# Fused delta-rule attention and two mixture-of-experts layers: sums of weight quarters on VectorE, and a sparser, reordered weight preparation

## The chip, the cores and the metric

The kernel runs on one core of a Trainium2 chip. The metric is the device time of one execution in microseconds (us). The engines are named as the profile names them: PE is TensorE (matmuls; PEld its weight loads), DVE is VectorE, ACT is ScalarE, POOL is GpSimd, SP is SyncE, which issues most of the DMAs. Each engine works through a queue of its own in order.

## The reference

Three stages follow each other on 4 sequences of 768 tokens (3072 tokens, 384 features):

```python
for t in range(S):                                  # delta-rule attention, 8 heads of 48
    y[:, :, t] = q[:, :, t] @ state
    state = state + beta * outer(k_n[:, :, t], v[:, :, t] - k_n[:, :, t] @ state)
...
logits = x @ w_gate                                 # MoE 1: soft routing, Sinkhorn, 8 experts
P = exp(logits - logits.max())                      # 8 times normalised over rows and columns
for e in range(E):
    out += P[:, e:e + 1] * (maximum(x @ w1[e], 0.0) @ w2[e])
...
expert_idx = argmax(xn @ en.T / tau, axis=1)        # MoE 2: one expert for each token
for e in range(E):
    out[mask] = gate_w[mask, None] * (maximum(x[mask] @ w1[e], 0.0) @ w2[e])
```

w1 is 384 x 1024 and w2 is 1024 x 384 for each expert. MoE 1 sends every token through every expert.

## The kernel before

The program has three parts in time. Part 1 (0 to about 560 us) is the attention with the experts 0 and 1 of MoE 1 woven in; a scheduler class orders it. Part 3 (from about 1664 us) is expert 7 of MoE 1, the routing and MoE 2; the scheduler orders it too. The change touches neither. It touches part 2, the experts 1 (rest) to 6 of MoE 1, whose order is written out by hand:

- **Foreground.** Every fp32 value is held as two fp16 halves, high and low, and a product takes three matmuls (high x high, high x low, low x high). First come the last groups of expert 1 (`moe1_group`, `mlp1`, `mlp2`, run by `run`), where PE works on L468 (first layer) and L479 (second layer), DVE makes the low halves of the hidden values on L452 and adds results to `accb` on L494. Then come 60 **units**: 12 blocks of 256 tokens for each of the experts 2 to 6. A unit has a first half (`blocks_first`: four blocks of 18 matmuls, L534) and a second half (`blocks_second`: seven products of 12 matmuls, L584), made Strassen-like from quarters of the hidden block and of w2. `turned` interleaves the first half of unit u with the second half of unit u-1: block, two products, block, two products, block, two products, block, one product.
- **Work on DVE, ACT and POOL for a unit.** ACT makes relu and high halves (L542, L543, L519), DVE the low halves from PSUM (L544) and from SBUF (L522), POOL four sums of hidden quarters (L525), and DVE adds finished products into `accb` (L566, L570). A product whose operand or whose PSUM bank isn't ready stops PE, whose queue is in order.
- **Background.** `bg()` advances every queue in `bgs` by one step, that is, up to the next `yield`. While units run, `paced` calls `bg()` each time 1050 ns of nominal matmul time have been written (14 steps to a unit); before that `run` calls it at every second matmul group. What a step writes goes into the engines' queues at that place.
- **What the background does.** One queue holds `first_accs` and then two `woven_group`s, which weight and sum the parts of experts 0 and 1 into `accb` (L601, L602; L624, L626). The other, `prepq`, holds weight preparations and a small `setup2` for MoE 2: `prep1(e)` prepares expert e of MoE 1 (e = 2 is `first_prep`, with a staging buffer of its own), `prep2(e)` expert e of MoE 2, which it writes to `w2d` in DRAM. `prep2` waits until both woven groups are done, because they share a buffer. `prep1(e + 1)` enters the queue behind the job in progress when the first unit of expert e has been written.
- **A preparation (`prep_w`)** loads w1 and later w2 into `st` (L351, L353), takes sums of squares (ACT, L394), turns them into one power of two for all partitions (DVE L397 to L399; `over_parts`: DVE writes a diagonal on L358, PE multiplies it by ones on L362, DVE takes the maximum on L364), and then splits w1 or w2 into high and low halves by `split_steps`: ACT writes the high half of one piece (L371), DVE the low half of the piece before (L374), one such pair to a step. For w2 of the experts 2 to 6 of MoE 1 the pieces are `quarters`: three quarters of 128x768 are split, then four differences of quarters are formed in place on POOL (L431), then the four results are split. A quarter's split has 768 elements per partition, the other pieces have 512.
- **The end of part 2.** After the last unit's first half, its remaining high and low halves are written in one go, then its second half, then what is left in `bgs`.

## Time and profile before

| | us |
|---|---|
| runs (3) | 2100.07, 2102.55, 2106.96 |
| median | 2102.55 |
| the profiled execution: time | 2101.38 |
| the profiled execution: span from first to last instruction | 2099.2 |
| PE busy in the span | 1985.6 (95%) |
| DVE, ACT, POOL busy | 1387.7 (66%), 1150.6 (55%), 602.3 (29%) |
| part 2, 696 to 1664 us: length, PE busy | 968.0, 945.5 |

PE is the bound nearly everywhere, so the profile is read as a list of PE's idle times: which wait ended each of them, and what the engine that PE waited for was doing just before. The instruction durations of DVE, as listed, overlap the next one by about 0.07 us; the distance between the starts of two instructions in a row is what one really occupies.

### The profile page before, as it was taken

What the parts mean: (1) busy time and instruction counts of PE and PEld (TensorE: products, weight loads), DVE (VectorE), ACT (ScalarE), POOL (GpSimd) and SP (SyncE); (2) the same over time, 40 slices, a digit from 0 to 9 for tenths busy, and PEclk for the clock granted to TensorE, in tenths of its full rate; (3) what the DMA queues carried; (4) which work ended last, traced back from release to release, by engine and by line L of the source; (5) the groups of instructions that cost most, each with busy time, mean ns of one, the idle gap of its engine ahead of it and who ended that gap; (6) DMA issues with size and microseconds to landing.
All of it is one profiled execution on the core that took longest, in us unless ns stands there. A gap on an engine that the chain in (4) does not pass through costs nothing. (4 is left out here: it accounts for less than half of the span.)

```text
span 2099.2 us, 55384 instructions
## 1 busy us (share of the span) xinstructions
PE 1985.6 (95%) x23391; PEld 1630.9 (78%) x23391; DVE 1387.7 (66%) x3045; ACT 1150.6 (55%) x2374; POOL 602.3 (29%) x524
## 2 busy tenths in 40 slices
PE   3779999999999999999999999999999999999998
PEld 3667777777775479999899989988999755567777
DVE  6988988988772776776767677676766555551111
ACT  6766665666532656666666656665665333433322
POOL 2232233223100123533533343353333201022211
PEclk9889999999999999999999999999999999999999
DMA  8355655546535113022032112302220010168765
GB/s 281 82 104 107 126 114 110 123 103 132 116 100 208 45 61 121 32 92 91 31 121 96 58 54 99 121 32 91 95 88 31 1 28 20 31 222 332 251 222 208
DMA packets 325982, 230.02 MB, mean 110 GB/s; under 512 B 258572, under 2 KB 303536, under 8 KB 319330
## 3 DMA queue, kind: packets, MB, share of 16 engines
q1 hardware_dynamic: 321442, 216.18, 34.7%
q0 software_dynamic: 4288, 10.25, 1.4%
q8 instruction: 185, 3.03, 0.6%
q14 instruction: 67, 0.55, 0.1%
HBM read 146.94 MB, written 50.36 MB: 94 GB/s over the span
## 5 line engine op out<-in xcount | busy, mean ns | idle before, releaser
L534 PE MATMUL pt<-big,W 128*128 128x256 f16 x4320 | 511.0, 273 | 0.0
L534 PEld LDWEIGHTS <-W 128*128 128x128 f16 x4320 | 418.5, 98 | 43.9 <-issue 0.3
L542 ACT ACTIVATE R<-pt 128x512 f32<-128x512 f32 x240 | 142.6, 594 | 306.9 <-PE pt L534 283.4
L525 POOL TENSOR_TENSOR R<-R,R 128x512 f32<-128x512 f32 x120 | 155.3, 1294 | 371.6 <-ACT R L542 288.2
L566 DVE SCALAR_TENSOR_TENSOR accb<-py,pet,accb 128x192 f32<-128x192 f32 x240 | 123.0, 513 | 203.8 <-PE py L584 203.3
L525 POOL TENSOR_TENSOR R<-R 128x512 f32<-128x512 f32 x120 | 161.6, 1346 | 195.3 <-ACT R L542 190.6
L584 PEld LDWEIGHTS <-A 128*128 128x128 f16 x2520 | 211.1, 98 | 7.2 <-DVE A L522 2.6
L1089 PE MATMUL pt<-accb,W 128*128 128x256 f16 (+1 forms) x1368 | 180.9, 272 | 3.5 <-ACT accb L729 1.8
L1115 PE MATMUL py<-W,hhl 128*128 128x384 f16 x756 | 152.6, 328 | 2.6 <-ACT yo L1125 1.7
L584 PE MATMUL py<-W,A 128*128 128x192 f16 x1440 | 134.7, 246 | 2.1 <-DVE accb L566 1.4
L1089 PEld LDWEIGHTS <-W 128*128 128x128 f16 x1368 | 118.3, 100 | 18.7 <-issue 3.8
L1635 PEld LDWEIGHTS <-W 128*128 128x128 f16 x1008 | 90.6, 98 | 51.1 <-issue 0.7
L584 PEld LDWEIGHTS <-hhl 128*128 128x128 f16 x1440 | 120.6, 98 | 5.9 <-DVE hhl L522 3.6
L1655 PE MATMUL py<-W,hhl 128*128 128x384 f16 x624 | 108.8, 326 | 0.0
L1641 DVE SCALAR_TENSOR_TENSOR ttb<-pt,ttb 128x512 f16<-128x512 f32 x50 | 34.6, 692 | 111.5 <-ACT ttb L1640 111.1
L584 PE MATMUL py<-W,hhl 128*128 128x192 f16 x1080 | 105.1, 246 | 2.8 <-DVE hhl L522 2.7
L1115 PEld LDWEIGHTS <-hhl 128*128 128x128 f16 x864 | 74.2, 98 | 40.8 <-DVE hhl L1102 3.2
L394 ACT ACTIVATE jk<-st 128x512 f32<-128x512 f32 x162 | 98.0, 605 | 13.7 <-DMA st<-in_moe_w_dram 11.4
L584 PE MATMUL py<-ew,A 128*128 128x192 f16 x1080 | 104.3, 246 | 0.6 <-DVE A L522 0.5
L522 DVE TENSOR_TENSOR A<-R,A 128x512 f16<-128x512 f32 x120 | 100.7, 841 | 2.9 <-ACT A L519 2.9
L584 PEld LDWEIGHTS <-ttb 128*128 128x128 f16 x1080 | 91.0, 98 | 9.9 <-issue 5.4
L1635 PE MATMUL pt<-big,W 128*128 128x512 f16 x432 | 97.7, 379 | 0.0
(411 smaller groups left out, 4090.4 us busy)
## 6 DMA issues: line engine op xcount, KB each, us to landing
st<-in_moe_w_dram SPq DMA_DIRECT2D x27, 1536.0 KB, 9.9
W<-w2d SPq DMA_DIRECT2D x18, 1536.0 KB, 8.2
w2d<-big SPq DMA_DIRECT2D x16, 1536.0 KB
big<-w2d SPq DMA_DIRECT2D x8, 1536.0 KB, 7.4
accb<-w2d SPq DMA_DIRECT2D x8, 1536.0 KB, 8.1
big<-accb SPq DMA_DIRECT2D x90, 128.0 KB, 3.6
accb<-in_kq_dram SPq DMA_DIRECT2D x23, 448.0 KB, 4.6
st<-PTc SPq DMA_DIRECT2D x42, 128.0 KB, 3.2
```

The source lines that it names most:

```text
L394: nc.scalar.activation(out=jk, in_=st[:, c * CW:c * CW + CW], func=AF.Square, scale=2.0 ** 0.5, accum_out=ss[:, c:c + 1])
L522: return lambda: nc.vector.tensor_tensor(out=A[2 * k + 1], in0=src, in1=A[2 * k], op=ALU.subtract)
L525: nc.gpsimd.tensor_tensor(out=out, in0=a, in1=b, op=op)
L534: nc.tensor.matmul(out=po, lhsT=w1v(W, wv, kk, f), rhs=xv[:, kk].rearrange("p (h n) -> p h n", h=2), start=kk == 0 and x == 0 and f % 2 == ...
L542: nc.scalar.activation(out=(R1, R)[y][:, :, o:o + 256], in_=pv if y else pv_, func=AF.Relu)
L566: nc.vector.scalar_tensor_tensor(out=acc[t][:, sl], in0=src, scalar=sc, in1=acc[t][:, sl], op0=ALU.mult, op1=ALU.add)
L584: nc.tensor.matmul(out=py, lhsT=A[2 * ka + a_][:, 128 * q_:128 * q_ + 128], rhs=B[2 * kb + b_][:, DH * q_:DH * q_ + DH], start=first and q ...
L1089: nc.tensor.matmul(out=o[g4][:, nt_ * j:nt_ * j + nt_], lhsT=w1v(W, wv, kk, f_), rhs=XR[:, xv, kk], start=(kk == 0 and x == 0), stop=(kk = ...
L1115: nc.tensor.matmul(out=o["py", j][:, 0:DM], lhsT=a_[f_ // per][:, c_:c_ + 128], rhs=w2v(W, b_, f_), start=(f_ == 0 and x == 0), stop=(f_ = ...
L1635: nc.tensor.matmul(out=po, lhsT=w1v(W, wv, kk, f), rhs=xv[:, kk, :], start=(kk == 0 and x == 0), stop=(kk == KD - 1 and x == 2))
L1641: V((f"rs{q_}", id_), lambda q_=q_: nc.vector.scalar_tensor_tensor(out=HL[q_], in0=o[q_], scalar=0.0, in1=HH[q_], op0=ALU.max, op1=ALU.sub ...
L1655: nc.tensor.matmul(out=o["py"][:, 0:DM], lhsT=a_[f // per][:, c_:c_ + 128], rhs=w2v(W, b_, f), start=(f == 0 and x == 0), stop=(f == KF - ...
```

## The change

- The four differences of w2 quarters move from POOL (`gpsimd`) to DVE (`vector`), and the four empty steps behind them go.
- For experts 3 to 6 the quarter splits stand two steps apart instead of one (`more=1`); for expert 2 they stay one step apart.
- In `over_parts` the matmul comes one step later after the diagonal.
- In the woven groups each sum is followed by three steps instead of one, and the next load by ten instead of six. In `setup2` the transposes come two steps later.
- `prep1(3)` now stands in the queue right behind `setup2`, ahead of `prep2(0)`, and waits there until the first unit has been written (`open_`); the later ones enter as before.

```diff
--- before.py
+++ after.py
@@ -358,12 +358,13 @@
         nc.vector.tensor_scalar(out=dg, in0=I128, scalar1=m1, scalar2=c_, op0=ALU.mult, op1=ALU.mult)
         yield 1
         yield 1
+        yield 1
         pm = psm.tile([128, 128], F32, name="pmx", tag="m1")
         nc.tensor.matmul(out=pm, lhsT=one16, rhs=dg, start=True, stop=True)
         yield 1
         nc.vector.tensor_reduce(out=ma, in_=pm, op=ALU.max, axis=AX.X)
 
-    def split_steps(parts, s):
+    def split_steps(parts, s, more=0):
 
         for n_ in range(len(parts) + 1):
             if n_ < len(parts):
@@ -372,7 +373,8 @@
             if n_:
                 src, hi, lo = parts[n_ - 1]
                 nc.vector.scalar_tensor_tensor(out=lo, in0=src, scalar=s, in1=hi, op0=ALU.mult, op1=ALU.subtract)
-            yield 1
+            for _ in range(1 + more):
+                yield 1
 
     def prep_w(w1, w2, e, W, iv, stages, dst=None, wt=None, mats=None):
         half = WCOLS // 2
@@ -409,7 +411,7 @@
             else:
                 Wd, o = W, 0
             if i and mats is not None:
-                yield from quarters(st, mats, s)
+                yield from quarters(st, mats, s, 0 if apart_ else 1)
             else:
                 yield from split_steps([(st[:, c * CW:c * CW + CW], *(
                     Wd[:, wcol(i, c, part) - o:wcol(i, c, part) - o + CW] for part in range(2))) for c in range(NCH)], s)
@@ -419,20 +421,18 @@
         nc.vector.scalar_tensor_tensor(out=iv, in0=ps_[0], scalar=0.25, in1=ps_[1], op0=ALU.mult, op1=ALU.mult)
         yield 1
 
-    def quarters(st, mats, s):
+    def quarters(st, mats, s, more):
 
         q_ = st.rearrange("p (x f y d) -> p x y f d", x=2, f=FH, y=2)
         b11, b12, b21, b22 = (q_[:, x, y] for x in range(2) for y in range(2))
 
         def to(k, src):
             return (src, *(mats[2 * k + part].rearrange("p (f d) -> p f d", f=FH) for part in range(2)))
-        yield from split_steps([to(k, src) for k, src in enumerate((b11, b21, b22))], s)
+        yield from split_steps([to(k, src) for k, src in enumerate((b11, b21, b22))], s, more)
         for out, a, b in ((b11, b12, b11), (b12, b22, b12), (b22, b22, b11), (b21, b21, b22)):
-            nc.gpsimd.tensor_tensor(out=out, in0=a, in1=b, op=ALU.subtract)
+            nc.vector.tensor_tensor(out=out, in0=a, in1=b, op=ALU.subtract)
             yield 1
-        for _ in range(4):
-            yield 1
-        yield from split_steps([to(k, src) for k, src in ((3, b11), (5, b12), (4, b22), (6, b21))], s)
+        yield from split_steps([to(k, src) for k, src in ((3, b11), (5, b12), (4, b22), (6, b21))], s, more)
 
     def w1v(W, part, kk, f):
         o = (f // FH) * 3072 + part * 1536 + kk * 512 + (f % FH) * 128
@@ -625,12 +625,13 @@
             for x in range(2):
                 nc.vector.scalar_tensor_tensor(
                     out=acc[t], in0=yw[x, g][:, t % 4], scalar=pe[x][:, t:t + 1], in1=acc[t], op0=ALU.mult, op1=ALU.add)
-                yield 1
+                for _ in range(3):
+                    yield 1
             yield 1
         if g + 1 < GW:
             woven_load(0, y0d, g + 1)
             woven_load(1, y1d, g + 1)
-            for _ in range(6):
+            for _ in range(10):
                 yield 1
         woven[0] += 1
 
@@ -1446,8 +1447,8 @@
         yield 1
         er = yield from inv_norm(ess, 1, 8)
         nc.vector.tensor_scalar(out=ench, in0=ench, scalar1=er, scalar2=None, op0=ALU.mult)
-        yield 1
-        yield 1
+        for _ in range(4):
+            yield 1
         pt_ = psm.tile([128, KD, E], F32, name="pen", tag="m1")
         for kk in range(KD):
             nc.tensor.transpose(out=pt_[:, kk], in_=ench[:, 128 * kk:128 * kk + 128], identity=cs[0:8, 0:8])
@@ -1517,6 +1518,13 @@
     queue([], first_accs(), *(woven_group(g) for g in range(GW)))
     queue(prepq, iter([1] * 3), first_prep)
     queue(prepq, setup)
+    open_ = []
+
+    def prep1_3():
+        while not open_:
+            yield 1
+        yield from prep1(3)
+    queue(prepq, prep1_3())
     for e in range(E):
         queue(prepq, prep2(e))
     def paced(main, ns):
@@ -1581,8 +1589,10 @@
             paced(first_of(u), BGNS)
             paced(second_of(NG - 1), BGNS)
         if new_:
-            prepq.insert(min(1, len(prepq)), prep1(e + 1))
-            queue(prepq)
+            open_.append(e)
+            if e > 2:
+                prepq.insert(min(1, len(prepq)), prep1(e + 1))
+                queue(prepq)
     while early or late or lows:
         take(lows, early, late, late)
     paced(second_at(len(units) - 1), BGNS)
```

In the listings below, taken from the built programs, line numbers are those of each program's own file; in the changed one L375 is the low half of a split (L374 before), L433 the difference of quarters (L431), L421 the end of a preparation (L419). A row is operation, output<-inputs and size.

DVE, the last group of expert 1 before the units, where expert 2's w2 is prepared. `stb` is its staging buffer, W_96 its weights, `hhl` the hidden values, `py` the PSUM bank of a second-layer result. Before:

```order
L452 SCALAR_TENSOR_TENSOR hhl<-pt,hhl 128x512
L626 SCALAR_TENSOR_TENSOR accb<-big,pet,accb 128x384
L374 SCALAR_TENSOR_TENSOR W_96<-stb,w1s,W_96 128x768
L452 SCALAR_TENSOR_TENSOR hhl<-pt,hhl 128x512
L626 SCALAR_TENSOR_TENSOR accb<-big,pet,accb 128x384
L374 SCALAR_TENSOR_TENSOR W_96<-stb,w1s,W_96 128x768
L494 SCALAR_TENSOR_TENSOR accb<-py,pet,accb 128x384
L626 SCALAR_TENSOR_TENSOR accb<-big,pet,accb 128x384 x2
L494 SCALAR_TENSOR_TENSOR accb<-py,pet,accb 128x384
L626 SCALAR_TENSOR_TENSOR accb<-big,pet,accb 128x384
L494 SCALAR_TENSOR_TENSOR accb<-py,pet,accb 128x384
```

And now:

```order
L452 SCALAR_TENSOR_TENSOR hhl<-pt,hhl 128x512
L375 SCALAR_TENSOR_TENSOR W_96<-stb,w1s,W_96 128x768 x2
L494 SCALAR_TENSOR_TENSOR accb<-py,pet,accb 128x384
L626 SCALAR_TENSOR_TENSOR accb<-big,pet,accb 128x384
L375 SCALAR_TENSOR_TENSOR W_96<-stb,w1s,W_96 128x768
L433 TENSOR_TENSOR stb<-stb 128x4x192
L494 SCALAR_TENSOR_TENSOR accb<-py,pet,accb 128x384
L433 TENSOR_TENSOR stb<-stb 128x4x192 x2
L494 SCALAR_TENSOR_TENSOR accb<-py,pet,accb 128x384
L626 SCALAR_TENSOR_TENSOR accb<-big,pet,accb 128x384
L433 TENSOR_TENSOR stb<-stb 128x4x192
L494 SCALAR_TENSOR_TENSOR accb<-py,pet,accb 128x384
```

The third split, the differences (four L433, before on POOL) and the splits behind them stand between the L494 rows, and three of the five L626 shown (the woven sums) have gone further back; the last L452 of the group stands ahead of all splits.

In the units, at the differences for expert 4: POOL before (L525 are the unit's own sums, R its hidden blocks):

```order
L525 TENSOR_TENSOR R_15165<-R_15165 128x512
L431 TENSOR_TENSOR st<-st 128x4x192 x4
L525 TENSOR_TENSOR R_15165<-R_15165,R 128x512
L525 TENSOR_TENSOR R<-R,R_15165 128x512
L525 TENSOR_TENSOR R<-R 128x512
```

DVE before, from a unit's first L566 through the second group of splits:

```order
L566 SCALAR_TENSOR_TENSOR accb<-py,pet,accb 128x192
L522 TENSOR_TENSOR hhl<-R_15165,hhl 128x512
L544 SCALAR_TENSOR_TENSOR A_15162<-pt,A_15162 128x256
L522 TENSOR_TENSOR ttb<-R,ttb 128x512
L374 SCALAR_TENSOR_TENSOR W_96<-st,w1s,W_96 128x768
L374 SCALAR_TENSOR_TENSOR ew_14615<-st,w1s,ew_14615 128x768
L566 SCALAR_TENSOR_TENSOR accb<-py,pet,accb 128x384
L522 TENSOR_TENSOR ttb<-R,ttb 128x512
L374 SCALAR_TENSOR_TENSOR ew_14615<-st,w1s,ew_14615 128x768
L566 SCALAR_TENSOR_TENSOR accb<-py,pet,accb 128x192
```

DVE now, at the differences:

```order
L375 SCALAR_TENSOR_TENSOR W_96<-st,w1s,W_96 128x768
L570 SCALAR_TENSOR_TENSOR accb<-py,pet,accb 128x384
L544 SCALAR_TENSOR_TENSOR A_15158<-pt,A_15158 128x2x256
L433 TENSOR_TENSOR st<-st 128x4x192 x3
L566 SCALAR_TENSOR_TENSOR accb<-py,pet,accb 128x192
L433 TENSOR_TENSOR st<-st 128x4x192
L522 TENSOR_TENSOR A_15158<-R_15160,A_15158 128x512
L544 SCALAR_TENSOR_TENSOR hhl<-pt,hhl 128x256
L522 TENSOR_TENSOR A_15158<-R,A_15158 128x512
```

The differences have left POOL's queue, where they stood ahead of a unit's sums, and three stand on DVE in a row and a fourth behind one L566, all ahead of the two L522 that make the next operands.

DVE at the end of part 2, the last unit. L570 adds the last product of the unit before. Before:

```order
L566 SCALAR_TENSOR_TENSOR accb<-py,pet,accb 128x384
L522 TENSOR_TENSOR ttb<-R_15165,ttb 128x512
L544 SCALAR_TENSOR_TENSOR hhl<-pt,hhl 128x2x256
L570 SCALAR_TENSOR_TENSOR accb<-py,pet,accb 128x384
L544 SCALAR_TENSOR_TENSOR hhl<-pt,hhl 128x2x256
L522 TENSOR_TENSOR hhl<-R_15165,hhl 128x512
L522 TENSOR_TENSOR ttb<-R,ttb 128x512 x2
L566 SCALAR_TENSOR_TENSOR accb<-py,pet,accb 128x192
L566 SCALAR_TENSOR_TENSOR accb<-py,pet,accb 128x384
```

And now:

```order
L375 SCALAR_TENSOR_TENSOR big<-st,w1s,big 128x512 x3
L566 SCALAR_TENSOR_TENSOR accb<-py,pet,accb 128x384
L522 TENSOR_TENSOR ttb<-R_15161,ttb 128x512
L544 SCALAR_TENSOR_TENSOR hhl<-pt,hhl 128x2x256
L375 SCALAR_TENSOR_TENSOR big<-st,w1s,big 128x512 x2
L570 SCALAR_TENSOR_TENSOR accb<-py,pet,accb 128x384
L544 SCALAR_TENSOR_TENSOR hhl<-pt,hhl 128x2x256
L375 SCALAR_TENSOR_TENSOR big<-st,w1s,big 128x512
L522 TENSOR_TENSOR hhl<-R_15161,hhl 128x512
L522 TENSOR_TENSOR ttb<-R,ttb 128x512 x2
L566 SCALAR_TENSOR_TENSOR accb<-py,pet,accb 128x192
```

Six splits of the last preparation, `prep2(7)`, now stand between the last unit's rows, one of them just ahead of its L522; before, that preparation had ended nearly four units earlier.

## Rows read from the trace of the kernel before

**Rows 1.** Part 2 as one stretch: length, busy us (x instructions) by engine, PE's clock, DMA.

```profile
696.00:1664.00 968.00, 945.53 (x9663) 864.83 (x9662) 679.36 (x1217) 593.38 (x1250) 358.89 (x260) 1.00 0.20 72
```

**Rows 2.** PE's waits in 696:1664: who waited for whom, total us, times, longest.

```profile
PE py L584 <- DVE accb L566: 5.9, 6, 1.8
PE pmx L362 <- DVE btok L358: 3.6, 8, 1.2
PE py L479 <- DVE hhl L452: 2.8, 1, 2.8
...
PE pen L1453 <- DVE yo L1448: 1.4, 1, 1.4
```

**Rows 3.** Stretches of the quarter preparations, experts 2 to 6 (engines PE, PEld, DVE, ACT, POOL).

```profile
720.00:740.00 20.00, 15.00 (x81) 7.67 (x80) 17.81 (x21) 7.90 (x14) 7.62 (x4) 1.00 0.10 29
873.50:896.50 23.00, 23.00 (x245) 21.69 (x243) 21.13 (x29) 14.61 (x24) 16.73 (x9) 1.00 0.01 2
1004.50:1029.50 25.00, 22.91 (x237) 20.65 (x236) 22.53 (x28) 14.82 (x25) 14.95 (x9) 1.00 0.01 2
1200.50:1225.50 25.00, 22.28 (x229) 20.05 (x228) 22.43 (x28) 14.30 (x25) 15.72 (x9) 1.00 0.01 2
1396.50:1421.50 25.00, 22.28 (x232) 20.45 (x229) 22.13 (x28) 13.62 (x23) 16.64 (x10) 1.00 0.00 1
```

**Rows 4.** Timeline of DVE, four places: start, duration, what, how many.

```profile
720.39 1.02 DVE L374 SCALAR_TENSOR_TENSOR W<-stb,w1s,W 128x768 f16<-128x768 f32 x1
...
723.64 2.56 DVE L374 SCALAR_TENSOR_TENSOR W<-stb,w1s,W 128x768 f16<-128x768 f32 x1
...
728.71 4.02 DVE L626 SCALAR_TENSOR_TENSOR accb<-big,pet,accb 128x384 f32<-128x384 f32 x2
...
843.48 0.68 DVE L522 TENSOR_TENSOR ttb<-R,ttb 128x512 f16<-128x512 f32 x1
844.08 0.28 DVE L364 TENSOR_REDUCE w0p<-pmx 128x1 f32<-128x128 f32 x1
...
1014.55 2.05 DVE L522 TENSOR_TENSOR ttb<-R,ttb 128x512 f16<-128x512 f32 x1
1016.52 0.68 DVE L544 SCALAR_TENSOR_TENSOR hhl<-pt,hhl 128x512 f16<-128x512 f32 x1
...
1605.94 0.15 DVE L419 SCALAR_TENSOR_TENSOR ivt<-w0p,w1p 128x1 f32<-128x1 f32 x1
```

**Rows 5.** Timeline of POOL, two of these places (in brackets: idle before, and releaser).

```profile
721.50 3.89 POOL L431 TENSOR_TENSOR stb<-stb 128x768 f32<-128x768 f32 x2 [114.78 <-DVE W L374]
728.43 3.88 POOL L431 TENSOR_TENSOR stb<-stb 128x768 f32<-128x768 f32 x2 [3.04 <-DVE W L374]
...
1014.24 1.81 POOL L431 TENSOR_TENSOR st<-st 128x768 f32<-128x768 f32 x1 [0.96 <-DVE W L374]
```

**Rows 6.** Timeline of PE, three places; its listed ends are modelled.

```profile
726.86 4.24 PE L479 MATMUL py<-W,hhl 128*128 128x384 f16 x25 [2.79 <-DVE hhl L452]
...
838.17 1.15 PE L584 MATMUL py<-ew,hhl 128*128 128x192 f16 x12
839.16 2.13 PE L534 MATMUL pt<-big,W 128*128 128x256 f16 x18
841.13 0.66 PE L584 MATMUL py<-W,hhl 128*128 128x192 f16 x6
842.18 0.23 PE L362 MATMUL pmx<-btok,c 128*128 128x128 bf16 x1 [0.39 <-DVE btok L358]
...
1656.93 1.00 PE L584 MATMUL py<-W,hhl 128*128 128x192 f16 x10 [0.90 <-DVE hhl L522]
1659.76 1.15 PE L584 MATMUL py<-ew,ttb 128*128 128x192 f16 x12 [1.83 <-DVE accb L566]
```

**Rows 7.** Groups by line and shape in part 2: count, busy us, mean ns, idle before.

```profile
L525 POOL TENSOR_TENSOR R<-R 128x512 f32<-128x512 f32 x120 | 161.6, 1346 | 195.3 <-ACT R L542 190.6
...
L374 DVE SCALAR_TENSOR_TENSOR W<-st,w0s,W 128x512 f16<-128x512 f32 x36 | 25.5, 743 | 1.9 <-ACT W L371 1.7
```

## Prediction

> **What bounds the kernel now.** I read the stretches first. Part 2, all that the change touches, lasts 968.0 us, of which PE works 945.5 [rows 1]; its clock is granted in full. So nothing here can give more than 22.5 us. Then PE's waits in that part [rows 2]: every large one is for DVE. Those for L358 are scattered over the preparations, those for L452 and for the constants of MoE 2 (L1453) stand before the units or in the first one. Most of the rest lies in the stretches where quarters of w2 are prepared [rows 3]: there PE loses 5.0 us (20.00 less 15.00) for expert 2, nothing for 3, then 2.1, 2.7 and 2.7 for 4 to 6, 12.5 us in all. DVE is busy 88 to 92% in these stretches, POOL 60 to 73% in the four inside the units.
>
> Why DVE is late there is seen instruction by instruction. A quarter's low half takes 1.02 us alone and 2.56 beside POOL's differences; two L626 take 4.02 [rows 4] while POOL runs two differences in 3.9 [rows 5]. For expert 4, POOL starts a difference at 1014.24 and ends at 1016.05; L522, begun at 1014.55, lasts until 1016.60, as if it had begun when POOL ended [rows 4, 5]. The Trainium skill ("SBUF — State Buffer", SBUF: two separate sides) says that the port pair which these two engines share is an exclusive lock, held for a whole instruction; this trace agrees, with 2.05 us against 0.68.
>
> So PE pays less for DVE's own work than for DVE held up behind POOL, and for unit sums (L525) held up in POOL's queue behind the differences.
>
> **What the change costs and gives, part by part.** In a row of DVE an instruction occupies about 0.07 us less than is listed: L522 at 843.48 lists 0.68, the next begins 0.60 later [rows 4]. I use such occupancies: L522 and L452 0.60, a quarter split 0.93, L494, L626 and L566 of full width 0.53 (listed 0.6).
>
> *A difference on DVE* doesn't occur before. Lower bound: L522 is the same operation with 512 elements, 0.60 free; a split costs 1.02 - 0.743 = 0.28 more with 768 elements than with 512 [rows 4, 7]; so 0.87. Upper bound: held up for a whole unit sum of POOL, 1.35 [rows 7], so 2.2. I take 0.87 where POOL's queue has nothing, and up to 1.8 where the order puts it beside unit sums.
>
> *Expert 2.* No units run yet, so POOL, rid of the differences, does nothing, and all of DVE is at free prices. In the order now the last L452 stands ahead of all splits, so the 2.79 us wait for it [rows 6] goes. After it, up to the second L494, DVE has three splits, two L494, one L626 and one difference: 2.8 + 1.6 + 0.9 = 5.3 us. PE needs the bank that this L494 frees for its fourth result, that is, three results after it began the first (2.0 us each: 25 matmuls in 4.24 [rows 6]), 5.9. DVE starts on this row some 1.5 us after PE begins the first, so PE waits 5.3 + 1.5 - 5.9 = 0.9. From there to the first L452 of the next group stand three differences 2.6, two L494 and two L626 2.1, two splits 1.9 and L452 0.6, 7.2 us, against 5.9 until PE needs what it frees: 1.3. So 2.2 remain of 5.0. Bounds 1 and 4. **Gain 2.8.**
>
> *Experts 3 to 6.* Two opposite things: seven splits and all unit sums lose POOL's differences, and splits stand two steps apart; but DVE gets four differences in four steps. I add up DVE's row from the order and compare with the moment at which PE wants the operand: a block of 18 takes 1.97 us (839.16 to 841.13), a product 0.99 [rows 6]. Expert 4, shown above: at the unit's start the three unit sums run on POOL, 4 us. DVE's L570 and L544 end 1.2 us in, the first difference is held up to 2.9, the next two end at 4.2 and 5.1, L566 at 5.4, the fourth at 6.3, L522 at 6.9. Its operand is wanted after a block, two products and a block, in the third matmul: 6.1. PE waits 0.8 to 0.9. The same sum for experts 3, 5 and 6, where the differences stand elsewhere in the unit, gives 0.5, 0.8 and 0.65. To each I add a margin of 0.4 for what the sum leaves out between engines: 4.5 remain of 7.5. Lower bound 0.5 in all (no difference meets a unit sum); upper bound 22 (in each stretch two more differences and one or two splits are held up by a whole unit sum, 2.6 + 1.8, all of it on PE). I take 4.5, because POOL without differences has four unit sums of 1.3 us in a unit of 14.8, a third of the time [rows 7]. **Gain 3.0.**
>
> *The diagonal's product one step later.* PE waited eight times for L358, 3.6 us, at most 1.2 [rows 2]. A step is 1.05 us of matmuls, so the unit's own matmuls cover all but 0.15 of each; what comes behind, the maximum and the splits, has no deadline. Were the cover gone, the 3.6 would stay. **Gain 3.3.** The transposes of `setup2` come two steps later: the 1.4 us wait [rows 2] goes, **1.4**.
>
> *Woven sums spread out.* Sixteen L626 as before, eleven of them now in the first units, where 0.53 us each mostly fits into DVE's gaps; some stand beside the splits of `prep1(3)`'s w1. Between 0 and 1.5; **cost 0.3**.
>
> *Preparations that wait, and added steps.* `open_` is a matter of the order in which the program is written; no engine waits on it. Behind it stands `prep2(0)`, which nobody needs before part 3, and expert 3 is needed only twelve units later. `prep1(3)` loads some 1.5 us later than `prep2(0)` did, with nothing on SP's queue that PE needs sooner; 26 products and four quarter sequences (9 steps more, 4 fewer) add 46 steps of 1.05 us: 50 us in all. Before, the last preparation ended at 1605.9 [rows 4], 58 us ahead of the units' end near 1664, so it still ends inside. But its last six splits now stand in the last unit (order, above), where PE already waits 0.90 and 1.83 us for L522 and L566 [rows 6]. The split just ahead of L522 costs DVE 0.67 to 1.8, partly while it would have waited for POOL's sums anyway. **Cost 0.6** (0 to 2).
>
> *The splits of 512 elements.* Part of the wait for L566 [rows 2] belongs to them, and hangs on where in a unit they fall; the added step moves each half by one. I expect as many as before: 0, with 2 either way.
>
> Sum: 2.8 + 3.0 + 3.3 + 1.4 - 0.3 - 0.6 = 9.6 us. Against the profiled execution, 2101.4, that is 2091.8; it lay 1.2 below the median of the runs, so I forecast 2093.0 (0.45% less).
>
> **The rivals.**
>
> *A. DVE becomes the bound in the quarter stretches.* It is 88 to 92% busy there [rows 3] and gets more to do. At the upper bound experts 3 to 6 cost 22 us in place of 7.5; expert 2 still gives 2.0, L358 and L1453 give 4.7, the end takes 2: 9.8 slower, 2112. It is slower than before from 3.1 us to a stretch, by over 0.3% from 4.6. For: for expert 4 the order puts three differences right behind the unit sums. Against: a split alone takes 1.02, and POOL's share falls from two thirds to a third.
> A rule of the Trainium skill ("Perfetto Trace Analysis", Optimizing Scalar/DVE Operations) speaks for A: where DVE is saturated, it may pay to offload work to other engines, GpSimd included, though it warns that these two share a port. By its first half the differences belong on POOL and the sum is A's; by the rows on the lock it is the forecast's.
>
> *B. The place of the wait moves, its size stays.* The four differences take on DVE what the lock gave back, so in the units 7.5 stay, while expert 2, L358 and L1453 give 6 and the end takes 1.5: 2098, within 0.3%.
>
> *C. Nearly all of these stalls go:* no difference meets a unit sum. 4 + 7 + 3.5 + 1.4 = 16 us, 2086.5.
>
> **How the numbers follow.** A measurement of this kernel can tell 0.3%, 6.3 us, from no change; so faster means below 2096.2. Forecast (2089 to 2096) 0.45, B (2096 to 2104) 0.32, A 0.09, C 0.14. The range leaves out A, a tail of B and half of C: 2086 to 2103. Faster: the forecast's and C's, 0.58 with a little at the edge given to the same, 0.34; slower, most of A, 0.08.
>
> **What would show it.** No wait of PE for L452; waits for L358 below 0.5 us in all; a difference on DVE near 0.95 us listed where POOL is idle, up to twice that beside L525; quarter splits mostly at 1.0; PE idle 1 to 2 us in each quarter stretch; the last unit's two waits 3 to 4 us. I am wrong if PE idles over 3 us in a stretch (A), or if a difference on DVE takes well over 0.95 us free.

## The result, and the profile after

The changed kernel is slower: median 2116.56 us (2112.24 to 2122.14, six runs) against 2104.45 us (2100.07 to 2106.96, six runs) for the kernel before, a ratio of 1.0061 with a 95% interval of 1.0042 to 1.0079. The forecast was 2093.0, 0.45% faster. The profiled execution took 2115.12 us, 13.7 more than that of before; the rows below are its own, and lines are those of the changed kernel (L375 is the split's low half, L374 before; L433 the difference; L363 the diagonal's product; L406 the scale).

First the units of the kernel after as one stretch (from the first L534 to the last L584): its limits and length, then busy us (x instructions) of PE, PEld, DVE, ACT and POOL, the granted clock, and the share and rate of DMA.

```profile
739.40:1674.20 934.80, 907.31 (x9440) 845.89 (x9439) 668.91 (x1172) 565.63 (x1201) 323.87 (x240) 1.00 0.21 74
```

The same of the kernel before:

```profile
743.00:1664.00 921.00, 903.53 (x9441) 843.50 (x9440) 639.61 (x1156) 567.08 (x1200) 351.27 (x256) 1.00 0.21 73
```

The units begin 3.6 us earlier and last 13.8 us longer. Of these, 10.0 are idle time of PE (27.5 us, 17.5 before), and 3.8 are more busy time for the same matmuls, in good part a lower clock, as shown below. What follows the units, which the change doesn't touch, takes 439.1 us, 435.0 before; a later run of the changed kernel with one DMA moved has 435.30 there, so this is scatter.

PE's waits while the units run (743:1675), after:

```profile
PE py L584 <- DVE A L522: 6.8, 9, 3.0
PE py L584 <- DVE hhl L522: 6.1, 8, 1.7
PE py L584 <- DVE accb L566: 4.7, 6, 1.4
PE py L584 <- DVE A L544: 3.8, 2, 2.4
PE py L584 <- DVE ttb L522: 3.6, 9, 0.5
PE py L584 <- DVE hhl L544: 1.3, 1, 1.3
PE pmx L363 <- DVE btok L358: 0.9, 2, 0.6
```

Against [rows 2], the waits for L358 have fallen from 3.6 to 0.9 us and that for the constants of MoE 2 is gone, as intended. But the waits for L522, the low half of a hidden sum, are now 16.5 us in 26 places; in the same stretch before they were 5.5 in 11:

```profile
PE py L584 <- DVE hhl L522: 2.7, 3, 1.4
PE py L584 <- DVE ttb L522: 1.6, 5, 0.5
PE py L584 <- DVE A L522: 1.2, 3, 0.5
```

The stretches in which quarters are prepared, experts 2 to 6, which answer to [rows 3]: length, then PE's busy time.

```profile
720.00:740.00 20.00, 17.96 (x98) 9.34 (x97) 18.56 (x28) 10.61 (x16) 0.00 (x0) 1.00 0.00 0
828.00:853.00 25.00, 23.29 (x244) 21.61 (x243) 20.42 (x30) 12.22 (x22) 9.12 (x7) 1.00 0.18 65
1028.00:1053.00 25.00, 22.00 (x216) 20.48 (x215) 21.72 (x27) 12.42 (x22) 6.26 (x5) 0.93 0.01 1
1243.00:1268.00 25.00, 23.41 (x246) 21.60 (x244) 24.50 (x34) 13.60 (x24) 7.90 (x5) 1.00 0.03 5
1384.00:1409.00 25.00, 23.48 (x248) 21.84 (x246) 23.53 (x33) 15.21 (x27) 10.79 (x7) 1.00 0.05 7
```

Expert 2 loses 2.0 us in place of 5.0. Experts 3 to 6 lose 1.7, 3.0, 1.6 and 1.5, 7.8 in all: as much as before (7.5), only spread otherwise.

**Where the new waits come from.** They stand behind splits of 512 elements. The second half of expert 3 of MoE 2, DVE's timeline, and ahead of it the three sums of a new unit on POOL:

```profile
1175.65 2.62 POOL L525 TENSOR_TENSOR R<-R,R 128x512 f32<-128x512 f32 x2 [5.53 <-ACT R L542]
1178.34 1.60 POOL L525 TENSOR_TENSOR R<-R 128x512 f32<-128x512 f32 x1
1182.48 1.40 POOL L525 TENSOR_TENSOR R<-R 128x512 f32<-128x512 f32 x1 [2.54 <-ACT R L542]
```

```profile
1177.03 1.78 DVE L375 SCALAR_TENSOR_TENSOR big<-st,w1s,big 128x512 f16<-128x512 f32 x1
1178.74 1.76 DVE L375 SCALAR_TENSOR_TENSOR big<-st,w1s,big 128x512 f16<-128x512 f32 x1
1180.42 0.74 DVE L375 SCALAR_TENSOR_TENSOR big<-st,w1s,big 128x512 f16<-128x512 f32 x1
1181.08 0.41 DVE L566 SCALAR_TENSOR_TENSOR accb<-py,pet,accb 128x192 f32<-128x192 f32 x1
1181.41 0.74 DVE L375 SCALAR_TENSOR_TENSOR big<-st,w1s,big 128x512 f16<-128x512 f32 x1
1182.07 0.68 DVE L522 TENSOR_TENSOR hhl<-R,hhl 128x512 f16<-128x512 f32 x1
1182.67 0.41 DVE L544 SCALAR_TENSOR_TENSOR A<-pt,A 128x256 f16<-128x256 f32 x1
1183.01 1.42 DVE L522 TENSOR_TENSOR ttb<-R,ttb 128x512 f16<-128x512 f32 x1
```

And PE, with its idle time in brackets:

```profile
1182.81 1.00 PE L584 MATMUL py<-W,hhl 128*128 128x192 f16 x10 [0.87 <-DVE hhl L522]
1184.48 1.00 PE L584 MATMUL py<-ew,ttb 128*128 128x192 f16 x10 [0.51 <-DVE ttb L522]
```

Two splits beside POOL's sums take 1.78 and 1.76 us, and end 0.54 and 0.56 us after one of these sums; the third, begun when POOL had nothing more to do, takes 0.74. They and a fourth stand ahead of the two L522 whose results the unit's products want next, and the second L522 is itself held up by POOL's fourth sum (1.42 for 0.68). PE waits 0.87 and 0.51. A half earlier in the program that meets POOL idle (its sums end at 997.4 and begin again at 1003.74) shows the free price:

```profile
999.20 2.72 DVE L375 SCALAR_TENSOR_TENSOR W<-st,w0s,W 128x512 f16<-128x512 f32 x4
```

In this row one occupies DVE for 0.68 us (0.74 as listed), and PE waits for nothing. It is the lock of the prediction, which the Trainium skill ("SBUF — State Buffer", SBUF: two separate sides) states for two engines and whole instructions, here between a split and a unit sum; the trace agrees, 1.76 to 1.78 against 0.74.

**Which halves meet it** is settled by the program. A unit has 14 steps. In the kernel before a half without quarters took 28 steps, exactly two units, so the second half began where the first had: all halves of 512-element splits had their scale (L404 there) written at steps 1 to 7 of a unit, but for two at step 14. With the added step a half takes 29, and the halves walk through the unit: steps 8, 12, 13, 1, 2, 4, 8, 9, 11, 12, 14 and so on. "Place" below means this step. From the traces of the kernels before and after and of the first three experiments, PE's idle time from 2 to 26 us behind the scale, by place (without the first half of expert 3 where it runs beside the woven sums, and the changed kernel's last half, which runs into the end of the units):

| place | halves | PE idle, us |
|---|---|---|
| 1 | 10 | 0 to 1.08 |
| 2 to 7 | 46 | 0 in each |
| 8 | 8 | 0 to 0.28 |
| 9 | 11 | 1.25 to 1.68 |
| 10 | 6 | 1.45 to 1.95 |
| 11, 12 | 10 | 1.36 to 1.39 |
| 13 | 6 | 0.98 to 1.01 |
| 14 | 9 | 0.74 to 1.25 |

The kernel before has 1.6 us of it in all, the changed kernel 13.2. In the same halves the number of splits that list over 1 us, out of six, is none at places 2 to 5, at most one at 6 and 7, mostly two from 8 to 12, three at 13, mostly two at 14 and one at 1. So held-up splits and PE's waits go together, but not one for one: at place 8 two such splits cost at most 0.28, and two halves at place 10 lose 1.95 without any, where other work of DVE (the routing weights of a new expert) stands in the same spot. So what PE pays hangs also on what else is in DVE's queue and on how soon the L522 behind is wanted. No run took the unit sums off POOL, so that they are what holds the splits up is read from the traces; that the place decides is what the experiments test.

**Two more places.** For expert 4 the three first differences meet the unit sums on POOL, and a fourth sum holds up the L522 that PE wants. Of the three differences in the first row two list 2.04 and 1.91 beside the sums and the third 0.96. DVE, then PE, then two windows behind the wait (granted clock in the third column from the right):

```profile
1034.76 4.98 DVE L433 TENSOR_TENSOR st<-st 128x768 f32<-128x768 f32 x3
1039.66 0.41 DVE L566 SCALAR_TENSOR_TENSOR accb<-py,pet,accb 128x192 f32<-128x192 f32 x1
1039.99 0.95 DVE L433 TENSOR_TENSOR st<-st 128x768 f32<-128x768 f32 x1
1040.85 1.76 DVE L522 TENSOR_TENSOR A<-R,A 128x512 f16<-128x512 f32 x1
```

```profile
1042.67 1.61 PE L584 MATMUL py<-W,A 128*128 128x192 f16 x10 [3.00 <-DVE A L522]
```

```profile
1042.70:1046.00 3.30, 3.30 (x23) 3.14 (x24) 2.90 (x5) 0.00 (x0) 0.00 (x0) 0.53 0.00 0
1047.70:1052.70 5.00, 5.00 (x56) 4.75 (x54) 3.54 (x6) 2.85 (x5) 0.00 (x0) 1.00 0.02 3
```

After 3.00 us without a matmul the granted clock is 0.53 over 3.3 us, nearly all of it at the lower of its two levels (1.2 of 2.4 GHz), and full again from 1047.7. The second such place is the end of the units, where PE waits 1.3 and 1.7 us close together. What one such fall costs is seen in the two fastest kernels of the experiments below: both wait 0.86 and 1.8 us in the last unit, and the clock falls behind these waits in the kernel at place 7 with its loads in time, but not in the one at place 6. Behind the second wait, in this order:

```profile
1647.70:1651.00 3.30, 3.30 (x23) 3.07 (x23) 0.89 (x2) 0.00 (x0) 0.00 (x0) 0.55 0.00 0
1647.10:1650.40 3.30, 3.30 (x41) 3.30 (x41) 1.02 (x3) 0.00 (x0) 0.00 (x0) 1.00 0.00 0
```

23 matmuls in place of 41 in the same 3.30 us are 18 of 0.08, about 1.5 us for one fall. So about 3 of the 3.8 us would be the clock's by this estimate. It may be less: PE is busy longer in a kernel with more waits even where the clock doesn't fall, 905.5 us while the units run, 2.0 above before, in the kernel at place 7 with late loads (27.6 us idle, clock 1.00). And such waits don't always bring a fall, as the two rows show. In the changed kernel without the third step, below, a wait of PE of 3.00 us, again in a quarter stretch, is followed by this:

```profile
1446.00:1449.30 3.30, 3.30 (x36) 3.15 (x37) 3.30 (x7) 0.00 (x0) 0.00 (x0) 1.00 0.00 0
```

What decides between the two stays open.

Near 790 us DVE meets the woven sums, the splits of expert 3's w1 and POOL's sums (785.90 to 790.4) at once:

```profile
785.92 1.67 DVE L626 SCALAR_TENSOR_TENSOR accb<-big,pet,accb 128x384 f32<-128x384 f32 x1
787.51 3.43 DVE L375 SCALAR_TENSOR_TENSOR W<-st,w0s,W 128x512 f16<-128x512 f32 x2
790.87 0.61 DVE L570 SCALAR_TENSOR_TENSOR accb<-py,pet,accb 128x384 f32<-128x384 f32 x1
791.39 0.68 DVE L544 SCALAR_TENSOR_TENSOR A<-pt,A 128x512 f16<-128x512 f32 x1
```

The first row and the two splits behind it (1.75 and 1.76 us) are held up by POOL. PE waits 2.40 us for that L544.

### The profile page after: what moved, and what is told of

It is laid out like the page before. It is cut to its first block, busy times and chain, and to the rows that moved or that the text cites. A ratio compares the mean times of both kernels' runs of the same rounds, so it can differ in the third digit from the quotient of the medians.

```text
span 2113.3 us, 55371 instructions
## 1 busy us (share of the span) xinstructions
PE 1986.3 (94%) x23391; PEld 1629.6 (77%) x23391; DVE 1413.4 (67%) x3065; ACT 1148.9 (54%) x2374; POOL 566.9 (27%) x504
## 5 line engine op out<-in xcount | busy, mean ns | idle before, releaser
L534 PE MATMUL pt<-big,W 128*128 128x256 f16 x4320 | 511.2, 273 | 0.0
L534 PEld LDWEIGHTS <-W 128*128 128x128 f16 x4320 | 418.8, 98 | 43.8
L525 POOL TENSOR_TENSOR R<-R,R 128x512 f32<-128x512 f32 x120 | 158.1, 1317 | 415.9 <-ACT R L542 373.6
L525 POOL TENSOR_TENSOR R<-R 128x512 f32<-128x512 f32 x120 | 165.8, 1382 | 321.5 <-ACT R L542 178.3
L566 DVE SCALAR_TENSOR_TENSOR accb<-py,pet,accb 128x192 f32<-128x192 f32 x240 | 122.9, 512 | 172.4 <-PE py L584 172.1
L584 PEld LDWEIGHTS <-A 128*128 128x128 f16 x2520 | 212.0, 98 | 19.0 <-DVE A L522 9.5
L584 PE MATMUL py<-W,A 128*128 128x192 f16 x1440 | 136.0, 247 | 7.9 <-DVE A L522 5.8
L584 PEld LDWEIGHTS <-hhl 128*128 128x128 f16 x1440 | 121.1, 98 | 10.8 <-DVE hhl L522 7.9
L584 PE MATMUL py<-W,hhl 128*128 128x192 f16 x1080 | 106.0, 247 | 6.1 <-DVE hhl L522 6.1
L584 PE MATMUL py<-ew,A 128*128 128x192 f16 x1080 | 105.7, 247 | 4.8 <-DVE A L544 3.8
L396 ACT ACTIVATE jk<-st 128x512 f32<-128x512 f32 x162 | 97.9, 604 | 16.9 <-DMA st<-in_moe_w_dram 14.9
L584 PEld LDWEIGHTS <-ttb 128*128 128x128 f16 x1080 | 91.5, 98 | 11.5 <-DVE ttb L522 5.7
L522 DVE TENSOR_TENSOR A<-R,A 128x512 f16<-128x512 f32 x120 | 94.0, 785 | 8.1 <-ACT A L519 7.2
```

The costliest lines, as they stand in the source:

```text
L396: nc.scalar.activation(out=jk, in_=st[:, c * CW:c * CW + CW], func=AF.Square, scale=2.0 ** 0.5, accum_out=ss[:, c:c + 1])
L522: return lambda: nc.vector.tensor_tensor(out=A[2 * k + 1], in0=src, in1=A[2 * k], op=ALU.subtract)
L525: nc.gpsimd.tensor_tensor(out=out, in0=a, in1=b, op=op)
L534: nc.tensor.matmul(out=po, lhsT=w1v(W, wv, kk, f), rhs=xv[:, kk].rearrange("p (h n) -> p h n", h=2), start=kk == 0 and x == 0 and f % 2 == ...
L566: nc.vector.scalar_tensor_tensor(out=acc[t][:, sl], in0=src, scalar=sc, in1=acc[t][:, sl], op0=ALU.mult, op1=ALU.add)
L584: nc.tensor.matmul(out=py, lhsT=A[2 * ka + a_][:, 128 * q_:128 * q_ + 128], rhs=B[2 * kb + b_][:, DH * q_:DH * q_ + DH], start=first and q ...
```

## The experiments

The theory from the traces, P: the place of a half in the unit decides what its splits cost. Its rivals: the added step itself, or a half's length (S), and the differences, now on DVE (D). Ratios are to the kernel before.

**The added step alone.** Edit to the kernel before:

```diff
         yield 1
         yield 1
+        yield 1
         pm = psm.tile([128, 128], F32, name="pmx", tag="m1")
```

> The kernel before with one edit: the third empty step in over_parts, so that a half of a preparation takes 29 steps, not 28. Theory P (place in the unit): what the six splits of 512 elements of a half cost PE depends only on the step of a unit, of 14, at which the half's scale is written: by the two traces nothing at steps 2 to 7, 0.2 us at 8, 1.0 to 1.7 at 9 to 13, 0.8 at 14, about 0.3 at 1. Here the halves walk through all steps; added up 13.5 us of PE waits from such splits, against 1.6 before. The waits for L358 (3.6 us) go. So PE idles 26 to 28 us while the units run (17.5 before), and the time is 8 to 10 us above before. Theory D (the differences, now on DVE, and the wider spread make DVE late everywhere): none of that is in this kernel, so only the L358 waits go and it is about 3 us faster than before.

Measured: 2126.75 us, 1.0109 (1.0092 to 1.0126). PE idles 33.0 us while the units run. The splits of 512 elements cost 12.8 us, near the 13.5 that P has from the places, and the waits for L358 fall to 0.7. The time is worse than P said: quarters lose about 10 in place of 7.5 (they have moved too), the constants of MoE 2 hold PE up 4.1 us in the first unit in place of 1.4, and PE is busy 910.5 us in place of 903.5 (in part a lower clock). D falls: one step without any other edit brings the whole loss at the splits.

**Halves of 28 steps again, in two ways.** In the changed kernel, first without the third step, then with it but one step fewer behind the load:

```diff
-        yield 1
         pm = psm.tile([128, 128], F32, name="pmx", tag="m1")
```

> The changed kernel without the third empty step in over_parts: halves take 28 steps again, two units exactly. Theory S (the step itself does it: with 28 steps the splits hold a fixed place, as before, and cost little): the waits at splits of 512 elements fall from 13 to about 2 us, the waits for L358 return (3.6), and the time is 8 us below the changed kernel, about 2108. Theory P (only the place counts): the first halves now stand at steps 7, 9, 9, 10, 10, 11, 13, 13, 14, 14, later ones at 1 to 9; added up by the two traces 15 us of waits at such splits. With the waits for L358 back it is 3 to 6 us above the changed kernel, about 2120.

```diff
-                for _ in range(11):
+                for _ in range(10):
                     yield 1
```

> The changed kernel with ten steps in place of eleven behind each load: the diagonal's product keeps its late step and a half takes 28 steps. The halves stand at the same steps of the unit as in the changed kernel without the third step. Theory P: 15 us of PE waits at the splits of 512 elements, 13 in the changed kernel; waits for L358 stay below 1; time 0 to 3 us above the changed kernel. Theory S (a length of 28 steps is enough): about 2 us at such splits, 11 us below the changed kernel, 2105.

Measured: 2121.54 us, 1.0078 (1.0061 to 1.0095), and 2123.46 us, 1.0094 (1.0072 to 1.0116). S falls: neither gains; by the medians both are 5 to 7 us above the changed kernel, and PE idles 31.6 and 31.7 us in place of 27.5. Splits cost 15.0 and 18.0 us (15 expected; in the first 1.2, in the second 3.4 are from the first half of expert 3 beside the woven sums). A length of two units holds a half where it is, but here the first ones are held at places 9 to 14. The removal of the edit that began the loss makes it larger.

**The differences back on POOL, or alone on DVE.** The first is an edit to the changed kernel, the second to the kernel before; places are those of its base in each.

```diff
-            nc.vector.tensor_tensor(out=out, in0=a, in1=b, op=ALU.subtract)
+            nc.gpsimd.tensor_tensor(out=out, in0=a, in1=b, op=ALU.subtract)
```

> The changed kernel with one edit undone: the four differences of quarters run on POOL again, at the same steps. All steps and places are those of the changed kernel. Theory P: the waits at the splits of 512 elements stay as they are, 13 us; only the stretches of quarters move: expert 2 loses 5.0 us in place of 2.0, and the quarters of experts 3 to 6, 7.8 now, 7 to 12; so 2 to 7 us above the changed kernel. Theory D (the differences on DVE are what makes DVE late): the waits inside the units fall from 27.5 to about 17 us, and the time is some 10 us below the changed kernel.

```diff
-            nc.gpsimd.tensor_tensor(out=out, in0=a, in1=b, op=ALU.subtract)
+            nc.vector.tensor_tensor(out=out, in0=a, in1=b, op=ALU.subtract)
```

> The kernel before with one edit: the four differences of quarters on DVE, everything else and every step as before. The prediction's view (DVE is held up behind POOL): expert 2 loses 2 in place of 5.0 us, experts 3 to 6 lose 4 to 5 in place of 7.5, so 5 to 6 us faster. Theory P (the places decide, the engine of the differences little): expert 2 about 4, experts 3 to 6 about 7 to 9 us; within 2 us of before.

The first is the changed kernel's equal, 2116.61 us, 1.006 (1.0043 to 1.0077): expert 2 loses 2.8 in place of 2.0 (17.16 busy in the same 20 us), the quarters of experts 3 to 6 lose about 6 in place of 7.8, the splits as much as ever. So D falls again, and P's 2 to 7 us did not come. The second gains: 2100.32 us, 0.9975 (0.9963 to 0.9986). Its stretches of expert 2 and expert 6:

```profile
720.00:740.00 20.00, 17.80 (x94) 8.88 (x93) 17.20 (x28) 9.51 (x15) 0.00 (x0) 1.00 0.03 4
1396.50:1421.50 25.00, 23.76 (x250) 22.15 (x251) 23.66 (x35) 15.21 (x28) 8.65 (x6) 1.00 0.03 5
```

2.2 us remain for expert 2, and 1.5, 1.5, 1.3 and 1.2 for the others, 5.6 where there were 7.5. P's "within 2 us" is a miss, and the prediction's view of this edit (2 us for expert 2, 4 to 5 for the others, 5 to 6 us faster) is nearly right, at these places.

**All halves at one place.** If the place decides, a kernel that holds every half at place 7 should win. Edit to the changed kernel: ten steps behind a load, no last step of a preparation, one step fewer at the end of the quarters; then the same with POOL for experts 3 to 6, then that with the old woven spacing and order.

```diff
-                for _ in range(11):
+                for _ in range(10):
...
-            for _ in range(1 + more):
+            for _ in range(1 + (more if n_ < 4 else 0)):
                 yield 1
...
-        yield 1
+        if apart_:
+            yield 1
```

> The changed kernel with all lengths made whole units: ten steps behind each load, no last step of a preparation, one step fewer at the end of the quarters, so that a half takes 28 steps, a half with quarters 42, and all halves begin at step 7 of a unit, where five kernels showed no wait at splits of 512 elements beyond the first three units. Theory P: these waits fall from 13 to the 1 to 3 us beside the woven sums, quarters lose 1.45 each (measured at step 7), 5.8 in all; PE idles 14 to 15 us while the units run, 27.5 in the changed kernel. Time 2096 to 2100, below before by 4 to 8 us. Against P: if the place were only a companion of something else in the change, the time would stay above before.

> The same as the fixed places at step 7, with the differences of experts 3 to 6 on POOL (expert 2 keeps DVE). Theory P with what the POOL variant of the changed kernel showed (0.55 us at step 8, 1.33 at step 5 for a quarter stretch): 0.6 to 1.1 for each, 3.5 in all in place of 5.8; time 2094 to 2098, 2 us below the kernel with all differences on DVE. The prediction's view (POOL's sums hold DVE up): 1 to 4 us slower than it.

> As the one before, fixed places at step 7 and POOL for the differences of experts 3 to 6, and also the woven groups at their old spacing and the preparations in the old order (expert 0 of MoE 2 first, expert 3 behind it). If the wait of 2.5 to 3.4 us near 790 us is due to the woven sums standing beside the first half of expert 3, it goes here and the time is 2 to 3 us below the other one with POOL, 2092 to 2095. If it is only a matter of DVE's load in the first units, it stays.

All three lost: 2123.01 us, 1.0091 (1.0076 to 1.0106); 2129.75, 1.0122 (1.0107 to 1.0138); 2131.97, 1.0121 (1.0102 to 1.014). The parts foretold came true: behind the scale PE waits 0 to 0.2 us in every half at place 7 but the first half of expert 3 (3.4), which is 0 in the kernel with the old order, and a quarter stretch costs 1.45 with DVE, each of four. With POOL it costs 2.77, where I had expected 0.6 to 1.1: at an equal place the differences belong on DVE. The Trainium skill ("Perfetto Trace Analysis", Optimizing Scalar/DVE Operations) says that offloading from a saturated DVE to other engines, GpSimd among them, may pay, and cautions that these two share a port. The advice isn't borne out at this place, 2.77 us against 1.45; the caution is.

But some 20 us of waits had arisen *ahead* of the scales, which none of my numbers had. ACT's waits in the first of these kernels:

```profile
ACT jk L396 <- DMA st<-in_moe_w_dram: 45.0, 15, 3.9
```

In the changed kernel it is 14.9 us. ACT stands in its queue before the first sum of squares, whose load has not landed, with the relus of the unit behind it. I took the ten steps for the cause.

> The kernel with all halves fixed at step 7 of a unit, with eleven empty steps behind each load again in place of ten; to keep a half at 28 steps the empty step behind its last split goes, and everything starts 13 steps later, again at step 7. Theory L (ten steps are too few for the load: ACT stands in its queue before the first sum of squares, 45 us in 15 waits in that kernel, with the unit's relus behind it, and PE waits for those): ACT's waits for the load fall to 12 to 15 us, the waits of PE ahead of the second halves go, PE idles 11 to 15 us while the units run in place of 34.4, and the time is 2094 to 2100. Theory M (step 7 itself is a bad place for the sums of squares and the diagonal that stand ahead of it): PE still idles about 30 us, time about 2120.

Measured: 2114.34 us, 1.0056 (1.0041 to 1.0071). Inconclusive by its design: ACT still waits 41.4 us for loads and PE idles 27.6. To keep 28 steps I had cut the step behind the last split, so that from the last split, which frees `st`, to the first sum of squares there were eleven steps again, as in the kernels just seen, where before has twelve. The rows gave the better lead. SyncE, then ACT, then PE of this kernel, second half of expert 0 of MoE 2:

```profile
882.78 0.36 SPq L419 DMA_DIRECT2D w2d<-big  x1
883.23 0.38 SPq L353 DMA_DIRECT2D st<-in_moe_w_dram  x1
```

```profile
893.57 0.60 ACT L396 ACTIVATE jk<-st 128x512 f32<-128x512 f32 x1 [2.91 <-DMA st<-in_moe_w_dram]
```

```profile
901.05 0.50 PE L585 MATMUL py<-W,hhl 128*128 128x192 f16 x4 [0.65 <-DVE hhl L523]
902.98 1.00 PE L585 MATMUL py<-ew,ttb 128*128 128x192 f16 x10 [0.71 <-DVE ttb L523]
```

The load of 1536 KB goes out right behind a store of 1536 KB and is used 10.3 us later, at once when it lands. Only halves behind such a store wait; those behind a half that stores nothing don't. So the store was moved behind the load:

```diff
             if dst is not None:
-                nc.sync.dma_start(out=dst[:, half * i:half * i + half], in_=Wd)
+                stores.append((dst[:, half * i:half * i + half], Wd))
...
                 load_w(w1, w2, e, i, st)
+                store()
```

> The kernel with all halves fixed at step 7 and eleven steps behind the load, with one edit: the store to w2d is issued behind the next load in place of ahead of it. Read from its two forerunners: the stalls ahead of a half (two or three of 0.6 to 0.8 us of PE, 18 us in all) stand only behind halves whose store of 1536 KB goes out just ahead of the load, with eleven steps from the last split to the first sum of squares, where before and the changed kernel have twelve. Theory L (the load lands late because it shares the DMA engines with the store, ACT stands in its queue, the unit's relus behind it): ACT's waits for the load fall from 41 to under 15 us, PE idles 9 to 12 us while the units run in place of 27.6, time 2094 to 2100. Theory M (the sums of squares at steps 11 to 2 are in a bad place themselves): no change, 2114.

Measured: 2091.77 us, 0.993 (0.9912 to 0.9948). PE idles 10.0 us while the units run, and loads are no longer among the twenty largest waits of ACT. The same half, SyncE:

```profile
884.12 0.37 SPq L353 DMA_DIRECT2D st<-in_moe_w_dram  x1
884.59 0.52 SPq L384 DMA_DIRECT2D w2d<-big  x1
```

The first sum of squares is at 891.90, 7.8 us behind the load's issue, and waits for nothing. This kernel has every part of the change: differences on DVE, quarter splits two steps apart, the third step, the spread woven sums and the new order. What it adds is that all halves stand at place 7, and that the load isn't late. It is 0.7% faster than before where the change alone is 0.6% slower. So the place, with the load in time, decides over the sign; the place alone, with the load late, did not (1.0056 above).

**Does the late load have a share in the changed kernel's loss?** The changed kernel with only the store moved:

> The changed kernel with one edit: the store to w2d is issued behind the next load. All steps are the changed kernel's, so halves still walk through the unit. Theory P (its 13 us at the splits of 512 elements come from the place of the splits alone): they stay, 12 to 14 us, PE idles 26 to 28 us while the units run, 27.5 without the edit, time 2114 to 2118. Theory L2 (they too are due to loads that land late behind a store): they fall to under 4 us and the time to about 2103.

Measured: 2115.78 us, 1.0057 (1.004 to 1.0073).

```profile
742.20:1676.30 934.10, 907.09 (x9440) 845.79 (x9439) 666.41 (x1172) 565.60 (x1201) 323.20 (x240) 1.00 0.21 74
```

PE idles 27.0 us, and the splits cost 12.4 us in place of 13.2, inside P's 12 to 14: the late load has hardly a share in the loss at the splits; the place explains it.

**What the kernel before could gain at its own places.** Differences on DVE, the third step, the step behind the last split taken out in exchange, and `setup2` two steps later; then that with the differences on POOL; then the first of these with the store behind the load; and with all halves at place 6:

```diff
+        yield 1
         pm = psm.tile([128, 128], F32, name="pmx", tag="m1")
...
-            yield 1
+            if n_ < len(parts) or n_ == 3:
+                yield 1
```

> The kernel before with the four differences on DVE, the third step in over_parts, the empty step behind the last split removed in exchange (so a half stays at 28 steps), and the transposes of setup2 two steps later. Halves begin at steps 1 to 8 of a unit, with quarters at 8, 6, 5 and 4. Theory P: 0.5 us of waits at splits of 512 elements, quarters 5 to 6, L358 below 1, expert 2 about 2.2, the wait for the constants of MoE 2 gone: PE idles 9 to 11 us while the units run (17.5 before), 10 us less than before with expert 2's 2.8: 2092 to 2096. If P is wrong and the later product itself costs what the changed kernel lost, it lies above before.

> As the one with places kept and differences on DVE, but with the differences on POOL as before: only the third step in over_parts, its compensation, and setup2's two steps. Prediction's third and fourth term by themselves: the waits for L358 and for the constants of MoE 2 go, 3.3 and 1.4, waits at splits fall by 1; quarters as before at one step later, 6 to 9. 4 to 6 us faster than before, 2098 to 2100.

> The kernel with places kept and differences on DVE, with the store to w2d behind the next load. Theory L: the 2 us ahead of the second half of expert 0 of MoE 2 go, and the 2 to 3 us of late splits of expert 6 of MoE 2; PE idles 11 to 12 us while the units run in place of 15.1, and it is 3 to 4 us faster than that kernel, 2092 to 2094. Theory M: no change, 2096.

> The same with store behind load, and all halves begin at step 6 of a unit (halves of 28 steps, halves with quarters 42, one wait of 14 steps at the start). Theory P: no waits at splits of 512 elements; a quarter with differences on DVE at single steps lost 0.07 us at step 6 (once measured), so 0.3 for four, 5 to 6 before that; L358 below 1; the end 2.7. PE idles 4 to 7 us while the units run, 17.5 before; time 2085 to 2091. If the place explains only the waits at splits, not the quarters, the quarters keep 5 to 6 and it is about 2092.

Measured, in this order: 2096.32 us, 0.997 (0.9958 to 0.9981); 2104.49, 1.0002 (0.999 to 1.0014); 2096.73, 0.9949 (0.9929 to 0.9968); 2093.56, 0.9923 (0.9901 to 0.9944). PE idles 15.1, 17.1, 11.3 and 9.3 us while the units run. The second is a miss: the waits for L358 fall to 0.9 as foretold, but expert 2 loses 6.5 in place of 5.0, and one late load costs 2.0; the gain of the later product is real and was given back elsewhere. The first stays above the 9 to 11 us expected, by late loads (the 2.0 and 1 to 2 more) and by 3.0 for the quarters of expert 3 at place 8. The third shows these loads again: PE idles 3.7 us less, though the medians of the two are alike and only the ratios, each to the runs of before beside it, differ by 0.2%, with intervals that overlap. The fourth is, with the kernel at place 7, the fastest, and confirms P for quarters: at place 6 a quarter stretch costs 0.07 to 0.08 us, in each of four. It stays above the 4 to 7 us of idle time and the 2085 to 2091 expected; the runs of before beside it had a median of 2107.12, and the second halves cost 0.35 there, nine times, and PE waits in the first unit:

```profile
PE py L597 <- DVE hhl L557: 2.1, 6, 0.4
PE py L492 <- DVE accb L1552: 1.9, 1, 1.9
PE py L597 <- DVE A L557: 1.1, 3, 0.4
PE pen L1468 <- DVE yo L1461: 1.2, 1, 1.2
```

## Why the prediction was wrong

By its own steps, in us of PE time saved (+) or lost (-), all against [rows 2, 3]:

| step of the prediction | forecast | measured |
|---|---|---|
| expert 2 | +2.8 | +3.0 |
| experts 3 to 6, quarters | +3.0 | -0.3 |
| diagonal's product | +3.3 | +2.7 |
| `setup2` | +1.4 | +1.4 |
| woven sums spread | -0.3 | -2.5 |
| end of the units | -0.6 | -0.2 |
| splits of 512 elements | 0 | -11.6 |
| PE's busy time for the same matmuls (clock) | none | -3.8 |

Together -11.3. The units end 10.3 us later than before, and begin 0.7 earlier than expert 2's gain explains, so the rows account for all but 0.3.

**The step that failed** is "I expect as many as before: 0, with 2 either way." The sentence ahead of it had the right question: the waits "hang on where in a unit they fall; the added step moves each half by one". I took the place for a draw from the same urn. It wasn't: 28 is twice 14, and the kernel before held its halves at places where splits cost nothing. A step more is not a shift by one but the end of that hold: each half moves at least one further than the one before it, and the halves go through the whole unit, of whose 14 places six cost 0.7 to 2.0 us. The lengths were to be had beforehand, by counting the steps of `prep_w`, and a sign of the price from the held-up instructions of [rows 4, 5]. I applied the lock of DVE and POOL to differences and quarters, and not to the splits, although the unit sums stay on POOL whatever becomes of the differences.

**Expert 2** was right in mechanism and size: 2.2 foretold (0.9 and 1.3), 2.0 measured (0.74 and 1.30), 2.2 with that one edit alone. (With the differences on POOL and the rest of the change it is 2.8, so the steps around it helped as well.) A difference takes 0.95 us where POOL is idle, as said.

**Experts 3 to 6** were mis-sized, 7.8 where 4.5 were to remain; that is the size that rival B gave this part, and in expert 4 the mechanism of A, at 2.04 and 1.91 us for the two differences beside POOL's sums, within my bound of 2.2. The sum by the order for expert 4 gave 0.8 to 0.9 and it was 3.0: three differences took 4.98 us where that sum had 3.9 (1.2 to 5.1), and the L522 behind them was held by POOL's fourth sum, 1.76 as listed for 0.68, which I had left out. The engine wasn't the trouble: the same edit at before's places leaves 5.6, and at place 6 nearly nothing.

**The diagonal and `setup2`** were right. **The woven sums** had the right neighbour (splits of `prep1(3)`'s w1), and went past its bound of 1.5: two splits of 1.75 and 1.76 us and an L626 of 1.67, all beside POOL, for which PE waited 2.40. **The end** was right in size. **The clock** had no term, since before shows it full in this part; behind the wait of 3.00 us and in the last unit it fell.

**The rivals.** A's time, 2112, came near, but its reason, DVE short of time in the quarter stretches, explains only expert 4. None of the three had the cause.

## What to carry to other kernels

Where background work is dealt out in steps to a periodic foreground, work out the length of each job modulo the period before adding or removing a step: a job that happens to be a whole number of periods is held at one place, and an edit of one step anywhere turns this into a walk through all places, good and bad. Read what a job costs by its place, fix the place, and only then judge an edit; the change, slower by 0.6%, became 0.7% faster once its places were fixed and its loads came in time. And count such distances from the event that frees the buffer: a load behind a store of the same size landed too late for a job one step shorter.

## What the runs showed of the hardware

- As listed, a split of 512 elements on DVE takes 0.74 us alone and 1.75 to 1.78 beside a sum on POOL; a difference of 768 elements 0.95 to 0.96 and 1.91 to 2.04. The mean over a row of several hides this.
- A wait of PE of 3.00 us was followed by a granted clock of 0.53 for 3.3 us in the changed kernel, and by a full clock in the same kernel without the third step; waits of 0.86 and 1.8 us by 0.55 in the kernel at place 7 with its loads in time, and by a full clock in the one at place 6. PE had 23 matmuls in 3.30 us in the one case and 41 in the other, so where the fall comes it costs about 1.5 us beyond the wait (an estimate from these rows).
- A load of 1536 KB issued behind a store of the same size was used 10.3 us after its issue, with ACT waiting; issued ahead of the store, it was there 7.8 us after its issue, without a wait.
